# A spectral filter with a gated FFN on one core: scratch rows in another order, forward slabs closer together, Strassen sums on VectorE, and x added to twelve slabs by accumulating DMAs

## The chip, the core and the metric

The kernel runs on one core of one Trainium2 chip. The metric is the device time of one execution in microseconds (us), the median of several runs. The core has five engines with a queue of instructions each: TensorE (PE; its weight loads are listed as PEld), VectorE (DVE), ScalarE (ACT), GpSimd (POOL) and SyncE (SP), which here issues most of the DMAs. An engine works off its own queue in order; a wait of one instruction holds everything behind it on the same engine.

## The reference

`x` has 2048 rows of 640 columns (bf16). It is normalised by row, filtered in the frequency domain and multiplied by a gate from a feed-forward network; `x` is added at the end:

```python
xn = _layernorm(x, axis=-1)
X  = rfft2(xn);  X = X * (w_r + 1j * w_i);  s = irfft2(X, (S, D))      # S = 2048, D = 640, 321 columns kept
g  = silu((gelu(xn @ w_gate) * (xn @ w_up)) @ w_down)                  # F = 1536
return x + s * g
```

## The kernel before

The FFTs are matrix products. The 2048 rows are cut into 16 slabs (`NS`, index `n1`) of 128 rows, row = 16 * n2 + n1. A forward slab is two groups of instructions: `slab_S1` (product over n2 with Tfwd into `pz`, emptied by ScalarE) and, two steps later, `slab_D` (product over the columns with FT into `pd`, emptied by ScalarE into `RZ`), after which SP stores the slab to the DRAM scratch `ZDR` (L604). `load_B2` reads the scratch back in another order, so that the second transform over n1 can run as 64-row products: `s2_in(b)` gives `px`, ScalarE empties it into `xs`, VectorE multiplies it by the two filter tensors W1 and W2 (L659, into the buffers of `RZ`), and `s2_out(b)` gives `pu`, which ScalarE empties into `RX` (L680) and SP stores to the DRAM scratch `UDR` (L683). There are eleven such bursts (`BURSTS`). `load_V` reads `UDR` back (into VY for slabs 0 to 3 and over W2 for the others), and the inverse runs slab by slab: `gather` (L710), `slab_S1i` (pv), `group_Di` for three slabs at a time, `group_cs` and `group_Y` on VectorE, and `finish`, which multiplies a slab by its gate (L788), adds x from `RX` (L789) and lets SP store it (L790). The x rows come from `load_xt`, two slabs at a time, into two halves of `RX`.

The FFN is spread between these parts. `ffn_piece` (L806) is five products of 128x512 into a bank `psg` or `psu`; ScalarE applies gelu (L811) and VectorE multiplies the two (L813, into `UT`). The down product of the four groups of four slabs is done directly (`down_third`, L944) for group 0 and half of group 3, and for groups 1, 2 and half of 3 by a Strassen-Winograd scheme: `w_sum` and `u_sum` (L872, L881) make sums of the operands on VectorE, and `product(g, a, i)` makes seven products (L900) of six matrix multiplies each. What comes out of the banks is added up: on VectorE (L907), by ScalarE copies (L910, L919), and for two of the seven sums on GpSimd. `gated` applies the activation: for groups 1 and 2 by a tanh on ScalarE (L844) and a VectorE instruction (L849), both put off by one product each (`flush`).

The two pools of PSUM banks matter for the order: `psg` and `psu` have two banks each, used in turn by FFN pieces and products; `pz`, `pd`, `px`, `pu` and `pv` share two double banks.

The order of all of this is written out by hand. `back` is a list of 144 steps (FFN pieces, products, down thirds); `put(s, f, ...)` hangs other work behind step s. Steps 36 to 59 are the FFN of group 1, 60 to 71 its products, 72 to 95 the FFN of group 2, 96 to 107 its products, 108 to 131 the FFN of group 3, 132 to 137 its seven products and 138 to 143 its direct part. In the kernel before, `slab_S1` of slab n1 stands behind step `FA[n1]` (29 to 58), `load_B2` behind 60, the first `s2_in` behind 68, the last `s2_out` behind 90, `load_V` behind 91, and the first `slab_S1i` behind 100.

`TB` splits a `u_sum` over the six blocks of UT: the blocks below TB are summed during the FFN, the rest later, for the second half of a group (a = 1) inside the products.

## Time and profile before

| | us |
|---|---|
| median of 3 runs (lowest, highest) | 199.49 (199.12, 199.73) |
| the profiled execution: its own time | 198.94 |
| the profiled execution: its span | 197.2 |

The span is the time from the first to the last record of the profile; the run's own time holds what lies around it as well. The profile shows, by engine, when instructions ran and what they waited for: groups of instructions (busy time, mean ns of one, idle time before), waits (who waited for whom), the chain that ended last, a timeline, windows of time and the DMA issues with their time to landing. The TensorE clock was granted in full over the whole span. Lines such as L806 are lines of the kernel as printed above. The lines that matter stand in the prediction.

### The profile page before, as it was taken

To read this page: it belongs to the slowest core of one execution; us is meant where nothing else is said; L and a number is where in the kernel's file an instruction comes from. 1 tells how busy PE (TensorE), PEld (TensorE's weight loads), DVE (VectorE), ACT (ScalarE), POOL (GpSimd) and SP (SyncE) were. 2 spreads that over 40 slices of the span, in tenths; PEclk is the share of its full clock that TensorE was granted. 3 is DMA by queue.
4 is the path that set the end of the run, shared out by engine and by line. 5 is a ranking of instruction groups with operands and counts; after the bars stand their busy time and mean duration, and the time that the engine had idled before them with its cause. 6 is when DMAs were issued, how large, how long until landed. Compare 5 with 4: busy or idle time off the path is not lost.

```text
span 197.2 us, 4191 instructions
## 1 busy us (share of the span) xinstructions
PE 188.7 (96%) x1496; PEld 116.4 (59%) x1511; DVE 158.4 (80%) x380; ACT 127.6 (65%) x229; POOL 48.9 (25%) x78
## 2 busy tenths in 40 slices
PE   7999999999999999999899999997999999999992
PEld 5798854777555555676433433454765555557672
DVE  7887888989899877697786658566779887978994
ACT  4668567866976666825598878622766738374761
POOL 4448588997210200032200000002120000000310
PEclk9999999999999999999999999999999999999999
DMA  6999999676596773329953222329910416040713
GB/s 162 301 331 362 367 320 188 139 207 208 134 179 126 218 243 104 99 72 317 243 132 103 76 100 100 116 69 257 325 41 28 138 41 195 33 136 15 220 44 94
DMA packets 39653, 32.44 MB, mean 165 GB/s; under 512 B 13264, under 2 KB 38608, under 8 KB 39376
## 3 DMA queue, kind: packets, MB, share of 16 engines
q1 hardware_dynamic: 37568, 29.87, 54.7%
q10 hardware_dynamic: 1968, 0.98, 1.8%
q0 software_dynamic: 96, 1.31, 1.7%
q8 instruction: 12, 0.20, 0.4%
q14 instruction: 9, 0.07, 0.1%
HBM read 19.03 MB, written 7.88 MB: 136 GB/s over the span
## 4 chain that ended last, share of the span: by engine, by line
PE 81%; DVE 8%; DMA 3%; issue 3%; ACT 2%; SPq 1%; DVEq 0%; ACTq 0%
PE psg L806 26%; PE psu L806 25%; PE psu L900 5%; PE psg L900 5%; PE psu L944 3%; PE psg L944 3%; PE pz L565 2%; PE pu L674 2%; PE pv L730 2%; PE pd L596 2%; PE pd L575 2%; DMA VY<-UDR 2%; PE px L647 2%; DMA X<-in_A_x_dram 2%; DVE X L788 1%
## 5 line engine op out<-in xcount | busy, mean ns | idle before, releaser
L806 PE MATMUL psg<-XG,Wg 128*128 128x512 bf16 (+2 forms) x282 | 60.1, 342 | 0.7 <-issue 0.3
L806 PE MATMUL psu<-XG,Wu 128*128 128x512 bf16 (+2 forms) x283 | 60.2, 342 | 0.4 <-issue 0.2
L813 DVE TENSOR_TENSOR UT<-psu,ge 128x512 bf16<-128x512 f32 (+2 forms) x58 | 34.4, 593 | 18.4 <-PE psu L806 16.1
L811 ACT ACTIVATE ge<-psg 128x512 bf16<-128x512 f32 (+2 forms) x58 | 30.3, 523 | 16.8 <-PE psg L806 16.1
L806 PEld LDWEIGHTS <-Wu 128*128 128x128 bf16 x290 | 27.0, 98 | 22.4
L806 PEld LDWEIGHTS <-Wg 128*128 128x128 bf16 x290 | 25.9, 98 | 21.3 <-issue 3.5
L659 DVE TENSOR_TENSOR RZ<-xs,W 128x972 bf16<-128x972 bf16 (+2 forms) x22 | 14.0, 678 | 5.5 <-ACT xs L655 4.7
L900 PEld LDWEIGHTS <-UT 128*128 128x128 bf16 x150 | 14.3, 98 | 5.6 <-issue 0.2
L944 PEld LDWEIGHTS <-UT 128*128 128x128 bf16 x156 | 14.4, 98 | 5.0
L601 ACT CAST RZ<-pd 128x660 bf16<-128x660 f32 x16 | 11.3, 707 | 9.1 <-PE pd L598 9.1
L190 DVE BATCH_NORM_STATS2 st<-X 128x6 f32<-128x320 bf16 x32 | 14.0, 476 | 0.4 <-DMA X<-in_A_x_dram 0.4
L732 ACT CAST W<-pv 128x640 bf16<-128x640 f32 x16 | 11.0, 688 | 5.0 <-PE pv L730 4.8
L755 ACT ACTIVATE W<-pd 128x960 bf16<-128x960 f32 (+2 forms) x14 | 10.0, 778 | 5.1 <-PE pd L579 5.1
L680 ACT CAST RX<-pu 128x486 bf16<-128x486 f32 (+4 forms) x22 | 12.2, 557 | 0.3
L655 ACT CAST xs<-px 128x972 bf16<-128x972 f32 (+2 forms) x11 | 10.3, 935 | 3.2 <-PE px L647 3.2
L944 PE MATMUL psg<-Wd,UT 128*128 128x320 bf16 (+1 forms) x84 | 11.8, 288 | 0.0
L567 ACT CAST GEN<-pz 128x640 bf16<-128x640 f32 x16 | 11.2, 698 | 0.0
L907 POOL TENSOR_TENSOR Tfwd<-Y,XG 128x320 f32<-128x320 f32 x1 | 0.9, 868 | 40.0 <-ACT XG L919 40.0
L844 ACT ACTIVATE th<-Tfwd 128x320 f32<-128x320 f32 x10 | 4.5, 469 | 9.5 <-DVE Tfwd L907 9.5
L907 POOL TENSOR_TENSOR Tfwd<-XG,Tfwd 128x320 f32<-128x320 f32 x1 | 0.9, 857 | 38.3 <-ACT Tfwd L919 38.3
L944 PE MATMUL psu<-Wd,UT 128*128 128x320 bf16 (+1 forms) x72 | 10.3, 290 | 0.0
L761 DVE TENSOR_TENSOR W<-W 128x960 bf16<-128x960 bf16 (+1 forms) x12 | 7.3, 632 | 1.8 <-ACT W L755 1.8
(215 smaller groups left out, 317.1 us busy)
## 6 DMA issues: line engine op xcount, KB each, us to landing
ZDR<-RZ SPq DMA_DIRECT2D x32, 80.2 KB, 2.8
UDR<-RX SPq DMA_DIRECT2D x10, 240.8 KB, 2.4
RX<-in_A_x_dram SPq DMA_DIRECT2D x14, 160.0 KB, 2.6
B<-ZDR SPq DMA_DIRECT2D x8, 240.8 KB, 4.3
W<-UDR SPq DMA_DIRECT2D x4, 481.5 KB, 7.1
X<-in_A_x_dram SPq DMA_DIRECT2D x3, 640.0 KB, 10.0
Wd<-in_B_w_down_dram SPq DMA_DIRECT2D x1, 1920.0 KB, 14.3
out_dram<-VY SPq DMA_DIRECT2D x12, 160.0 KB, 1.8
```

Source lines behind the costliest of these rows:

```text
L190: nc.vector.bn_stats(out=st_n[n1][:, k, :], in_=X[:, n1, 320 * k:320 * k + 320])
L567: nc.scalar.copy(out=Zt[n1], in_=pz)
L601: nc.scalar.copy(out=zd.rearrange("p c (q e) -> p c q e", e=10), in_=pd[:, :, 0:330].rearrange("p c (e q) -> p c q e", q=33))
L655: nc.scalar.copy(out=xs, in_=px[:, :, 0:n * w].rearrange("p k (h l) -> p k h l", l=w))
L659: nc.vector.tensor_tensor(out=pp[-1], in0=xs, in1=WT[:, :, h0:h0 + n, l0:l0 + w], op=ALU.mult)
L680: nc.scalar.copy(out=us[:, :, :, c0:c0 + (w + 1 - m) // 2], in_=pv[:, :, :, m:w:2])
L732: nc.scalar.copy(out=vs, in_=pv)
L806: nc.tensor.matmul(ps, lhsT=WT[:, c, t * P:(t + 1) * P], rhs=xnT[g][:, c, c0:c1_], start=(c == 0), stop=(c == 4))
L811: nc.scalar.activation(out=ges[t], in_=ps, func=ACT.Gelu_apprx_tanh)
L813: nc.vector.tensor_tensor(out=UT[:, t, c0:c1_], in0=ps, in1=ges[t], op=ALU.mult)
L900: nc.tensor.matmul(ps, lhsT=lhs[:, t, :], rhs=rhs[:, t, :], start=(t == 0), stop=(t == 5))
L944: nc.tensor.matmul(ph, lhsT=UT[:, t, j * P:(j + 1) * P], rhs=Wd[:, t, c0:c1_], start=(t == 0), stop=(t == NT - 1))
```

## The change

- The scratch tensors lose their split by odd and even rows: `[2, 2, NS, 64, L]` becomes `[2, NS, P, L]`. A forward slab is stored by one DMA of 128 partitions (two of 64 before), and `load_V` issues four DMAs of 128 partitions (eight of 64 before). The rows of the second transform change places with it: B2 and the `RX` buffers hold the two halves `hh` of a row pair next to each other, and `load_B2` and the `UDR` stores are split by the upper and lower 64 partitions, with runs of 3852 bytes (128 partitions with runs of 1926 bytes before), in the same number of DMAs. In `w_plus` the rows read are every second one, so each of its DMAs moves 16 x 16 rows of 642 bytes (16 contiguous runs of 10272 bytes before). The constants follow (`u64`). The two `RX` buffers of the second transform are used in the other order.
- Forward slabs 8 to 15 stand closer: FA ends at 54 instead of 58, `slab_D` always two steps later. `load_B2` stands behind step 56 (60 before), the first `s2_in` behind 67 (68), the last `s2_out` still behind 90 but two steps after the last `s2_in`, `load_V` still behind 91, the first use of V one step earlier.
- The Strassen sums: products 3 and 4 change places, and all sums are made on VectorE from the bank; the second copy by ScalarE and the two sums on GpSimd go. `TB` is 5 instead of 3, and the sums of the operands stand at other steps.
- `finish` of slabs 0 to 11 (`XA` = 12) leaves out the VectorE add of x: GpSimd issues a DMA that adds x from DRAM to the slab (`accum_op=ALU.add`), and SP's store waits for it. `load_xt` remains for slabs 12 to 15.

```diff
-    ZDR = dram.tile([2, 2, NS, 64, L], BF16)
-    UDR = dram.tile([2, 2, NS, 64, L], BF16)
+    ZDR = dram.tile([2, NS, P, L], BF16)
+    UDR = dram.tile([2, NS, P, L], BF16)
...
     def w_plus(i, hh, lo):
-        u0 = lo * 32 + hh * 16
-        nc.sync.dma_start(out=WT[p0:p0 + 61:4, lo].rearrange("p h l -> p (h l)"),
-                          in_=sp[:, u0:u0 + NS, :].rearrange("k h l -> k (h l)"))
+        u0 = lo * 32 + hh
+        nc.sync.dma_start(out=WT[p0:p0 + 61:4, lo], in_=sp[:, u0:u0 + 31:2, :])
...
     def slab_D(n1):
-        for a in range(2):
-            nc.sync.dma_start(out=ZDR[a, :, n1].rearrange("c p l -> p c l"), in_=zd[a:P:2, :, 0:L])
+        nc.sync.dma_start(out=ZDR[:, n1].rearrange("c p l -> p c l"), in_=zd[:, :, 0:L])
...
+    def turned(t, lo, h0, h1):
+        return t[64 * lo:64 * lo + 64, 2 * h0:2 * h1, :].rearrange("p k l -> p (k l)")
+
+    def rows(t, lo, h0, h1):
+        v = t.rearrange("c n (z a k) l -> a (c n z) (k l)", a=2, z=2)
+        return v[lo, :, 2 * h0 * L:2 * h1 * L]
...
     def load_B2():
-            for hh in range(2):
-                nc.sync.dma_start(out=B4[:, hh, h0:h1, :], in_=zv[:, hh, h0:h1, :])
+            for lo in range(2):
+                nc.sync.dma_start(out=turned(B2, lo, h0, h1), in_=rows(ZDR, lo, h0, h1))
...
     def s2_out(b):
-        us = st_b["u"][:, h0 // 3 % 2, :, 0:n * L].rearrange("p k (h l) -> p k h l", l=L)
+        ut = st_b["u"][:, (h0 // 3 + 1) % 2, 0:2 * n, :]
+        us = ut.rearrange("p (h k) l -> p k h l", k=2)
...
-            for hh in range(2):
-                nc.sync.dma_start(out=uv[:, hh, h0:h0 + n, :], in_=us[:, hh, :, :])
+            for lo in range(2):
+                nc.sync.dma_start(out=rows(UDR, lo, h0, h0 + n), in_=turned(ut, lo, 0, n))
...
     def load_V():
             for c in range(2):
-                for a in range(2):
-                    nc.sync.dma_start(out=V[a:P:2, :, c * L:c * L + L],
-                                      in_=UDR[a, c, n0:n1].rearrange("n p l -> p n l"))
+                nc.sync.dma_start(out=V[:, :, c * L:c * L + L], in_=UDR[c, n0:n1].rearrange("n p l -> p n l"))
...
     def finish(n1):
-        nc.vector.tensor_tensor(out=Y, in0=Y, in1=xts[n1][:, sl], op=ALU.add)
+        if n1 < XA:
+            nc.gpsimd.dma_start(out=Y, in_=xv[:, n1, sl], accum_op=ALU.add)
+        else:
+            nc.vector.tensor_tensor(out=Y, in0=Y, in1=xts[n1][:, sl], op=ALU.add)
...
-    TB = 3
+    TB = 5
...
     def product(g, a, i):
-                    (A(1, 0), TS[:, 2]), (S[:, 0], TS[:, 0]), (A(0, 1), B4[:, :, 1, 1, :]), (A(1, 1), TS[:, 3]))[i]
+                    (S[:, 0], TS[:, 0]), (A(1, 0), TS[:, 2]), (A(0, 1), B4[:, :, 1, 1, :]), (A(1, 1), TS[:, 3]))[i]
...
         elif i == 3:
-            d["p7"], d["u3"] = temp(), temp()
-            nc.scalar.copy(out=d["p7"], in_=ps)
-            add(nc.gpsimd, d["u3"], d["p1"], d["p7"])
+            d["u4"] = temp()
+            add(d["u4"], d["p1"], ps)
         elif i == 4:
-            d["u4"] = temp()
-            add(nc.vector, d["u4"], d["p1"], ps)
-            add(nc.gpsimd, d["p7"], d["u4"], d["p7"])
+            c, d["u3"] = temp(), temp()
+            add(c, d["u4"], ps)
+            gated(g, j + 1, 1, c, True)
+            add(d["u3"], d["p1"], ps)
...
-    for i, at in enumerate((51, 52, 54, 56)):
+    for i, at in enumerate((51, 52, 53, 54)):
         put(at, w_sum, i)
-    put(52, u_sum, nc.vector, 1, 0, 0, 3)
-    put(57, u_sum, nc.vector, 1, 1, 0, 3)
-    put(59, u_sum, nc.vector, 1, 0, 3, 6)
...
+    for g, at in ((1, 56), (2, 92), (3, 128)):
+        put(at, u_sum, nc.vector, g, 0, 0, TB)
+        if g in STR:
+            put(at + 1, u_sum, nc.vector, g, 1, 0, TB)
+        put(at + 3, u_sum, nc.vector, g, 0, TB, 6)
-    FA = (29, 31, 33, 35, 37, 39, 41, 43, 45, 47, 49, 51, 53, 55, 57, 58)
+    FA = (29, 31, 33, 35, 37, 39, 41, 43, 44, 46, 47, 49, 50, 51, 53, 54)
     for n1 in range(NS):
-        put(min(FA[n1] + 2, 45 + n1), slab_D, n1)
+        put(FA[n1] + 2, slab_D, n1)
         put(FA[n1], slab_S1, n1)
-    z_end = F0 + 30
+    z_end = FA[NS - 1] + 2
...
-    sb = z_end + 8
+    sb = 67
...
-    put(sb + 22, s2_out, len(BURSTS) - 1)
-    sb += 23
+    put(sb + 23, s2_out, len(BURSTS) - 1)
+    sb += 24
     put(sb, load_V)
-    vs0 = sb + 8
+    vs0 = sb + 7
...
-    put(vs0 - 2, load_xt, 0)
-    put(vs0 + 4, load_xt, 1)
+    for pair in range(XA // 2, 8):
+        put(vs0 + 4 * pair, load_xt, pair)
```

More of the change, by code (lines that the diff above doesn't have):

```diff
@@ L119, in w_minus @@
         p0 = hh * 64 + 1
[L120 removed]
+        u0 = lo * 32 + hh
         if u0 == 0:
[L122 removed]
+            nc.sync.dma_start(out=WT[p0:p0 + 61:4, lo, 1:NS, :], in_=sp[:, 126:97:-2, :])
             nc.sync.dma_start(out=WT[p0:p0 + 61:4, lo, 0, :], in_=sp[:, 64, :])
         else:
[L125 removed]
+            nc.sync.dma_start(out=WT[p0:p0 + 61:4, lo, :, :], in_=sp[:, 128 - u0:97 - u0:-2, :])
     def w_twin(i, pm):
@@ L647, in s2_in @@
                     nc.tensor.matmul(ps, lhsT=MG[r, kind, 0, :],
-                                     rhs=B2[r, 16 * hh + h0 + i:16 * hh + h0 + j, l0:l0 + w], start=(i == 0),
+                                     rhs=B2[r, 2 * (h0 + i) + hh:2 * (h0 + j) - 1 + hh:2, l0:l0 + w], start=(i == 0),
                                      stop=(j == n))
@@ L660, in s2_in @@
         st_b[b] = pp
-    uv = UDR.rearrange("a c n (z k h) l -> (a c n z) k h l", z=2, k=2)
     def s2_out(b):
@@ L713, in gather @@
             st_c[("r", n0 + k)] = vr[:, k, :]
+    XA = 12
     xts = {}
@@ L906, in product @@
         j = 2 * a
-        add = lambda eng, out, in0, in1: eng.tensor_tensor(out=out, in0=in0, in1=in1, op=ALU.add)
+        add = lambda out, in0, in1: nc.vector.tensor_tensor(out=out, in0=in0, in1=in1, op=ALU.add)
         if i == 0:
@@ L1117, in build @@
             put(min(d + (5 + k if n == 3 else 2), vs0 + 41), finish, n0 + k)
-            if (n0 + k) % 2 and 1 < (n0 + k + 3) // 2 < 8:
-                put(min(d + (5 + k if n == 3 else 2), vs0 + 41), load_xt, (n0 + k + 3) // 2)
     warm_pe(21)
```

29 lines of the change are left out of this document (8 added, 21 removed).

## The prediction

> **What bounds the kernel now.** I read the page of the profile first: the share of each engine, the 40 slices, and the chain of work that ended last.
>
> ```profile
> span 197.2 us, 4191 instructions
> PE 188.7 (96%) x1496; PEld 116.4 (59%) x1511; DVE 158.4 (80%) x380; ACT 127.6 (65%) x229; POOL 48.9 (25%) x78
> PE   7999999999999999999899999997999999999992
> PE 81%; DVE 8%; DMA 3%; issue 3%; ACT 2%; SPq 1%; DVEq 0%; ACTq 0%
> ```
>
> TensorE is busy 188.7 of 197.2 us and holds 81% of the chain. The number of its matrix products does not change, so the change can only win back what TensorE stands still, 8.5 us, of which start and end take most: the slices dip at the first, at slice 28 (133 to 138 us) and at the last. Next come TensorE's own waits (us in total, times, longest).
>
> ```profile
> PE pv L730 <- DMA VY<-UDR: 1.3, 1, 1.3
> PE pu L674 <- ACT RX L680: 0.8, 2, 0.5
> ```
>
> Two waits stand out, and the chain in order of time (start, length, what) shows both places. The first is the entry to the second transform:
>
> ```profile
> 94.86 0.46 PE pu L674 x6
> 95.37 0.50 DVE Tfwd L907
> 95.95 0.47 ACT th L844
> 96.42 0.85 ACT xs L655
> 97.30 1.23 DVE RZ L659 x2
> ...
> 99.91 0.86 ACT xs L655
> ...
> 101.88 0.62 PE pu L674 x8
> ...
> 105.10 0.41 PE pu L674 x8
> ...
> 108.10 0.41 PE pu L674 x8
> ```
>
> From 105.10 on a burst and its two FFN halves take 3.00 us. The three bursts from 94.86 to 105.10 took 10.24 us, so 10.24 - 9.00 = 1.24 us are lost here. The chain says why: a VectorE sum of the Strassen products (L907) ends late, ScalarE stands in order behind the tanh that needs it, and so empties px and pu late. The second place is the load of V:
>
> ```profile
> 130.63 0.58 SPq L699
> ...
> 132.57 3.33 DMA VY<-UDR
> ...
> 136.03 0.53 PE pv L730 x4
> 136.56 0.81 PE psu L900 x6
> ```
>
> SP issues four loads one after the other, and only the fourth, under way at 132.57, ends the wait. Then the tail (start, length, engine, line):
>
> ```profile
> 192.66 0.83 PE L944 MATMUL psg<-Wd,UT 128*128 128x128 bf16 x12
> 193.53 0.28 ACT L841 ACTIVATE XG<-psg 128x128 bf16<-128x128 f32 x1 [0.34 <-PE psg L944]
> 194.23 0.22 DVE L789 TENSOR_TENSOR X<-X,RX 128x128 bf16<-128x128 bf16 x1
> ```
>
> TensorE ends at 193.5 and VectorE's last add at 194.45: the last 1 us is the inevitable last piece, and the store follows. A lighter VectorE does not shorten it. What can be won is thus 1.24 + 1.3 us and crumbs: about 3 us is the ceiling.
>
> **The change part by part, against the profiled execution (span 197.2, its own time 198.94; the median of the runs is 199.49, 0.55 above).**
>
> *Load of V.* Four VY loads of 64 rows become two of 128 rows, and four W2 loads two. Issue time on SP, by the tile view (min, median, max in ns), and, from the list of DMA issues, size and time to landing:
>
> ```profile
> L699 SPq DMA_DIRECT2D VY<-UDR x4: 605/616/646, 130.6 to 132.6; - x4
> UDR<-RX SPq DMA_DIRECT2D x10, 240.8 KB, 2.4
> UDR<-RX SPq DMA_DIRECT2D x2, 80.2 KB, 3.9
> ```
>
> Two issues fewer are 2 x 0.62 = 1.24 us less before the last VY load is under way. SP starts them when the last UDR stores have landed. The two small stores took 3.9 us against 2.4 for bigger ones, so I read 1.5 us as queueing behind the burst before; that burst's stores now go one step earlier, while the small ones stay at their step (90). Bounds of this: 0 to 1.5 us earlier. Against both, the first use of V moves one step forward (vs0 is 98, not 99): one product, 0.81 us, less cover. TensorE's wait becomes 1.3 + 0.81 - 1.24 = 0.87 us with no help from the stores and vanishes with 0.9 of it. A gain of 0.4 to 1.3; I take 1.0, near the upper end, since the step that now separates the stores is about half of the 3.00 us pace and covers most of the 0.9. What is late next is the gather on VectorE (L710), which waits for the same load and is issued one step earlier too; behind it stand two product sums whose banks TensorE needs only two products later, so this costs nothing.
>
> [...]
>
> *Entry to the second transform.* Forward slabs 8 to 15 come up to four steps earlier, so the B2 load is called at step 56 instead of 60 and s2_in(0) at 67 instead of 68; s2_in(1) and s2_out(0) come at step 70, ahead of the last two products rather than behind them. The load gains some three steps on its first reader, so it should no longer be the reader's limit. What remains is VectorE. Rows of one instruction each (count, busy us, mean ns, idle before):
>
> ```profile
> L907 DVE TENSOR_TENSOR Tfwd<-Tfwd,psg 128x320 f32<-128x320 f32 x4 | 1.9, 479 | 0.1
> L881 DVE TENSOR_TENSOR XG<-UT 128x384 bf16<-128x384 bf16 x6 | 2.1, 353 | 0.1
> L789 DVE TENSOR_TENSOR VY<-VY,RX 128x640 bf16<-128x640 bf16 x12 | 5.9, 492 | 0.4
> ```
>
> Each set of seven products has seven sums on VectorE instead of five: five sets, ten sums, 10 x 0.48 = 4.8 us more, of which 4 x 0.48 = 1.9 fall before this entry. Five ScalarE copies and ten GpSimd sums go. The GpSimd sums were not free to VectorE:
>
> ```profile
> 86.11 0.86 POOL L907 TENSOR_TENSOR FT<-Tfwd,Y 128x320 f32<-128x320 f32 x1 [17.39 <-ACT Y L919]
> 86.18 1.01 DVE L881 TENSOR_TENSOR UT<-UT 128x384 bf16<-128x384 bf16 x1
> ...
> 92.53 1.91 DVE L659 TENSOR_TENSOR RZ<-xs,W 128x972 bf16<-128x972 bf16 x2 [0.80 <-DMA B<-ZDR]
> 92.96 0.95 POOL L907 TENSOR_TENSOR Y<-Tfwd 128x320 f32<-128x320 f32 x1 [3.94 <-ACT Tfwd L919]
> ```
>
> Under a GpSimd sum the 0.35 us instruction took 1.01 and the 1.23 us pair 1.91: 0.66 + 0.68 = 1.3 us come back. The u_sums keep their elements, but with TB at 5 less of them lies inside the products: three of 384 columns become three of 128, at most 0.35 each and say 0.4 in all. Net on VectorE before the entry: +1.9 - 1.3 - 0.4 = +0.2 us. ScalarE has two copies less in its queue, and px(1) and pu(0) are emptied while sums are still to come, not behind the last tanh. Bounds: if neither the GpSimd relief nor the new order helps, 1.9 - 0.4 = 1.5 us lost; if the entry runs at the steady pace, 1.24 won. I take 0.6 won, since the row that names the wait (pu on ScalarE's RX) is the one that the new order attacks.
>
> In the second group the same sums meet two VectorE idles at the V loads, and four product banks stand between VectorE and TensorE; in the third, VectorE has lost more than it gained (next part). Both at nothing; without that cover a set costs 2 x 0.48 us.
>
> *x by an accumulating DMA.* Twelve VectorE adds of 0.49 (5.9 us) and twelve x loads go; twelve GpSimd DMAs come. TensorE shows no wait on VectorE there, so 5.9 us of VectorE are worth nothing by themselves: they pay for the sums above. The DMA itself has no row; the nearest are GpSimd's copies of W2:
>
> ```profile
> L129 POOL DMA_DIRECT2D W<-W x2 | 1.4, 686 | 12.2 <-DMA ZDR<-RZ 12.2
> W<-W POOLq DMA_DIRECT2D x2, 642.0 KB, 4.2
> 183.52 0.49 DVE L789 TENSOR_TENSOR VY<-VY,RX 128x640 bf16<-128x640 bf16 x1
> 189.59 5.32 SPq L790 DMA_DIRECT2D out_dram<-X  x8
> ```
>
> SP's store of a slab now waits for its DMA, and everything behind it on SP too: the x loads for slabs 12 to 15, which have over 10 us to spare, and the last stores. The last accumulated slab is multiplied by 183.5. With three issues of 0.69 and a landing of 4.2 it is home at 189.8, as the stores of slab 12 begin. Bounds: nothing, to 1 us if a landing takes twice 4.2 (194, when SP still has three stores to issue). I take 0.
>
> *Scratch rows in another order.* The forward store is one DMA for two; SP gains time nobody waits for. w_plus reads 16 x 16 rows of 642 bytes in place of 16 long ones. Windows of 1 us (window, length, then busy time of PE, PEld, DVE, ACT and POOL, PE clock, DMA share, GB/s), and the first reader of Tfwd:
>
> ```profile
> 26.00:27.00 1.00, 1.00 (x7) 0.46 (x5) 1.00 (x4) 0.23 (x1) 0.92 (x4) 1.00 1.00 394
> 29.00:30.00 1.00, 1.00 (x7) 0.44 (x5) 0.97 (x4) 1.00 (x2) 1.00 (x1) 1.00 1.11 214
> ...
> 36.83 5.15 SPq L361 DMA_TRANSPOSE Tfwd<-Tinv  x4
> ...
> 40.36 0.39 PE L565 MATMUL pz<-Tfwd,RX 128*128 128x128 bf16 x4
> ```
>
> Full DMA engines move 394 GB/s of long rows and 214 while the w rows run. Four w_plus of 160 KB are 1.6 us at the one and 3.0 at the other: up to 1.4 us more in front of the transposes of Tfwd, which are issued 3.5 us ahead of their first use. Bounds 0 to 1.4; I take 0.1.
>
> Sum: -1.0 - 0.6 + 0.1 = -1.5 us: span 195.7, profiled run 197.4, median 199.49 - 1.5 = 198.0.
>
> **The rivals.**
> 1. *Both waits go altogether.* 1.24 + 1.3 plus some tenths of scattered issue gaps: -2.8, 196.7. For it: after the entry the pace is steady. Against it: px must still be emptied by a ScalarE that waits for tanh inputs.
> 2. *The gain is hidden.* The 64-row stores land no sooner than before, or later, so that of the V load only 0.4 is left, and the entry stays as it was: -0.3, 199.2. For it: the use of V was moved forward by as much as two of the loads gave. [...]
> 3. *VectorE becomes the bound in the products (slower).* Place: the entry at 95 to 102. If VectorE reaches RZ of the third burst more than about 1 us later than now, pu(2) waits for it, and behind pu(2) the FFN. Price: 1.5 us as above, less what V gains shrink to (0.4 of it, as the later end of the stage holds the last stores too), and 0.3 to 0.5 in the second group: +1.4, 200.9. For it: VectorE's sums lie on the chain already. Against it: the collisions with GpSimd.
> 4. *The accumulating DMAs are slow (slower).* From a landing of about 8 us on, slabs 9 to 11 hold SP beyond 191 and the last stores queue: at 10 us some 2 us, less the 1.5 gained: 200.1. For it: SP serves in order. Against it: 160 KB is a quarter of what took 4.2 us.
>
> [...]
>
> **How the numbers follow.** Forecast 0.52, rival 1 0.14, rival 2 0.15, rival 3 0.12, rival 4 0.07. A measurement here tells no change up to 0.3%, 0.6 us. Faster: 0.52 + 0.14 = 0.66; within: 0.15; slower: 0.19. The forecast's own range is 196.9 to 198.9. Down to 196.3 most of rival 1 is in; up to 200.2 rival 2 and the milder half of the slower ones: 196.3 to 200.2.
>
> **What would show it.** Right: TensorE's wait at pv on VY under 0.4 us with two VY issues in front; the first three pu intervals summing to under 9.8 us; no GpSimd sum and no 1.0 us L881; VectorE's share near 79%. Wrong: SP's wait on UDR longer than before (rival 2); TensorE waiting on RZ or for a product bank (rival 3); out stores waiting on accumulating DMAs past 190 us (rival 4); a TensorE gap near 40 us (w rows). If nothing of this moves and the time does, the reasons are wrong.

## The result, and the profile after

| | changed kernel | kernel before, same chip | ratio (95% interval) |
|---|---|---|---|
| first measurement | 197.05 us median (196.43 to 197.27, 4 runs) | 199.31 us (199.00 to 199.73, 4 runs) | 0.988 (0.985 to 0.9911) |
| second measurement | 196.47 us (195.93 to 196.62, 6 runs) | 198.71 us (198.18 to 200.51, 29 runs) | 0.988 (0.985 to 0.991) |

The changed kernel is faster by 2.25 us, both times; the forecast was 1.5. Executions over 1.5% longer than the fastest of the same kernel are left out of every ratio here, but not out of the medians, and the one profile of v_both is of such an execution, so that its stages are not in the table below. The changed kernel's first profiled execution took 197.07 us (span 195.2), its second 196.40 (span 194.5). From the page of the first:

```profile
span 195.2 us, 4162 instructions
PE 187.4 (96%) x1496; PEld 115.6 (59%) x1511; DVE 154.5 (79%) x379; ACT 126.6 (65%) x224; POOL 50.5 (26%) x80
PE   7899999999999999999999999999999999999992
PE 80%; DMA 10%; SPq 3%; DVE 3%; ACT 2%; issue 1%; DVEq 0%; ACTq 0%
```

The dip of slice 28 is gone from TensorE's row, and VectorE has gone from 8% of the chain to 3%. The share of DMA rose from 3% to 10% (5% in the second profile), as the chain now passes through the B2 load, though TensorE shows no wait for it. TensorE's waits of the same profile (us in total, times, longest):

```profile
PE pt L973 <- DVE X L218: 0.8, 1, 0.8
PE pu L674 <- ACT RX L681: 0.4, 1, 0.4
PE pz L563 <- DMA Tfwd<-Tinv: 0.4, 1, 0.4
PE pv L730 <- DMA VY<-UDR: 0.3, 1, 0.3
```

The wait for V fell from 1.3 to 0.3 us and that at pu from 0.8 to 0.4. The wait at pz is new. The one at pt at the very start looks like a loss of 0.8 us and is none, as the timelines of TensorE of the first and of the second profile of the changed kernel show (start, length, engine, line):

```profile
1.18 3.83 PE L609 MATMUL psg<-GEN 128*128 128x256 bf16 x21 [1.18 <-DVE eps L229]
5.77 0.54 PE L973 MATMUL pt<-ident,X 128*128 128x128 bf16 x5 [0.77 <-DVE X L218]
```

```profile
1.17 4.66 PE L609 MATMUL psg<-GEN 128*128 128x256 bf16 x21 [1.17 <-DVE eps L229]
5.80 0.72 PE L973 MATMUL pt<-ident,X 128*128 128x128 bf16 x5
```

The same 21 warming products took 3.83 us in one execution and 4.66 in the other, and the first transposition starts at 5.8 in both: the wait is what the products left over.

To find where the 2.25 us come from, I cut TensorE's timeline at five instructions that every kernel here has: the first matmul of the forward transform (pz), the first product of each FFN group that is multiplied out in products (P1, P2, P3), and the last group of matmuls. The rows for the kernel before (the first and the last of the five stand in the prediction: 40.36 and 192.66):

```profile
81.83 0.98 PE L900 MATMUL psg<-Wd,UT 128*128 128x320 bf16 x6
...
130.45 0.98 PE L900 MATMUL psg<-Wd,UT 128*128 128x320 bf16 x6
...
178.63 0.98 PE L900 MATMUL psg<-Wd,UT 128*128 128x320 bf16 x6
```

and for the second profile of the changed kernel:

```profile
40.51 0.38 PE L563 MATMUL pz<-Tfwd,RX 128*128 128x128 bf16 x4
...
82.28 0.98 PE L903 MATMUL psg<-Wd,UT 128*128 128x320 bf16 x6
...
129.57 0.98 PE L903 MATMUL psg<-Wd,UT 128*128 128x320 bf16 x6
...
176.36 0.98 PE L903 MATMUL psg<-Wd,UT 128*128 128x320 bf16 x6
...
190.06 0.83 PE L946 MATMUL psg<-Wd,UT 128*128 128x128 bf16 x12
```

Differences of such rows give the length of each stage. The experiments of the next section are in the table too, each read in the same way from its own profile.

| kernel | span | to pz | pz to P1 | P1 to P2 | P2 to P3 | P3 to last group | rest |
|---|---|---|---|---|---|---|---|
| before | 197.2 | 40.36 | 41.47 | 48.62 | 48.18 | 14.03 | 4.5 |
| changed, first profile | 195.2 | 40.69 | 41.78 | 47.30 | 47.34 | 13.70 | 4.4 |
| changed, second profile | 194.5 | 40.51 | 41.77 | 47.29 | 46.79 | 13.70 | 4.4 |
| rows_only | 196.7 | 40.16 | 41.48 | 48.95 | 47.47 | 14.03 | 4.6 |
| acc_only | 196.7 | 40.48 | 41.48 | 48.63 | 47.66 | 14.03 | 4.4 |
| old_slots | 196.4 | 40.86 | 41.48 | 48.84 | 47.07 | 13.71 | 4.4 |
| rows_steps | 194.7 | 40.33 | 41.78 | 47.63 | 46.59 | 13.70 | 4.7 |
| old_sums | 194.5 | 40.37 | 41.77 | 47.64 | 46.59 | 13.71 | 4.4 |
| x_vector | 194.3 | 40.20 | 41.78 | 47.30 | 46.59 | 13.79 | 4.6 |
| v_halves | 195.3 | 40.88 | 41.78 | 47.30 | 47.45 | 13.71 | 4.2 |
| late_bursts | 195.2 | 40.59 | 41.77 | 47.39 | 47.29 | 13.71 | 4.4 |
| both_fixes | 194.9 | 40.49 | 41.77 | 47.29 | 47.27 | 13.71 | 4.4 |
| fixes2 | 194.5 | 40.40 | 41.78 | 47.30 | 46.88 | 13.71 | 4.4 |

Two columns repeat to a few hundredths of a microsecond: pz to P1 and P1 to P2. With the new steps the D of slab 15 stands before P1 rather than behind it; that moves 0.31 us from the one to the other (41.78 - 41.47) and is no gain. So the entry to the second transform, which lies between P1 and P2, won 48.62 - 0.31 - 47.30 = 1.01 us. P2 to P3, with the load of V, won 0.84 us in the first profile and 1.39 in the second; its floor, reached three times, is 46.59. P3 to the last group won 0.33. The start differs by scatter and by the wait at pz.

Nearly all of the 1.01 us lies at two places. One is the first burst, px(0), and no list of waits names it, since the row merges the products around the stop. TensorE's timeline, before and in the first profile of the changed kernel:

```profile
90.38 0.79 PE L647 MATMUL px<-B,MG 64*64 64x162 bf16 x5
91.10 0.99 PE L900 MATMUL psg<-X,UT 128*128 128x320 bf16 x6
```

```profile
89.90 0.41 PE L649 MATMUL px<-B,MG 64*64 64x162 bf16 x5
90.24 0.99 PE L903 MATMUL psu<-X,RX 128*128 128x320 bf16 x6
```

From px(0) to the product behind it are 0.72 us before and 0.34 after: 0.38 won. By the single records of the trace the third of the five products starts at 90.77, and the second B2 load, issued at 87.8, lands 2.9 us later, at 90.73: the kernel before did wait for that load. In acc_only, which has the same loads, px(0) takes 0.74. The other place is the distance of the first pu's, here in the first profile of the changed kernel:

```profile
93.02 0.58 PE L674 MATMUL pu<-RZ,N 64*64 64x162 bf16 x10
...
96.58 0.57 PE L674 MATMUL pu<-RZ,N 64*64 64x159 bf16 x10
...
100.19 0.63 PE L674 MATMUL pu<-RZ,N 64*64 64x486 bf16 x8 [0.45 <-ACT RX L681]
...
103.25 0.57 PE L674 MATMUL pu<-RZ,N 64*64 64x477 bf16 x8
```

From pu(0) to pu(3) are 10.23 us in both kernels (94.70 to 104.93 before, by the timeline), but the work between is not the same: the changed kernel has the last two products (1.63 us) there and one FFN half (1.08) less. At the steady pace of 3.00 this takes 9.00 us before and 9.00 + 1.63 - 1.08 = 9.55 after, so 1.23 were lost before and 0.68 after: 0.55 won. From pu(3) to the next are 2.99 us again.

### The profile page after: what moved, and what is told of

It is laid out like the page before. It is cut to its first block, busy times and chain, and to the rows that moved or that the text cites. A ratio compares the mean times of both kernels' runs of the same rounds, so it can differ in the third digit from the quotient of the medians.

```text
span 195.2 us, 4162 instructions
## 1 busy us (share of the span) xinstructions
PE 187.4 (96%) x1496; PEld 115.6 (59%) x1511; DVE 154.5 (79%) x379; ACT 126.6 (65%) x224; POOL 50.5 (26%) x80
## 4 chain that ended last, share of the span: by engine, by line
PE 80%; DMA 10%; SPq 3%; DVE 3%; ACT 2%; issue 1%; DVEq 0%; ACTq 0%
PE psu L809 25%; PE psg L809 24%; PE psg L946 5%; PE psg L903 4%; PE psu L946 4%; DMA B<-ZDR 4%; PE psu L903 3%; DMA VY<-UDR 2%; PE pz L563 2%; PE pd L573 2%; SPq L624 2%; PE pv L730 2%; PE pd L594 2%; PE pu L674 2%; DMA Tfwd<-Tinv 1%
## 5 line engine op out<-in xcount | busy, mean ns | idle before, releaser
L809 PEld LDWEIGHTS <-Wu 128*128 128x128 bf16 x290 | 26.1, 98 | 22.5 <-issue 3.4
L809 PEld LDWEIGHTS <-Wg 128*128 128x128 bf16 x290 | 26.5, 98 | 20.2 <-issue 0.2
L790 POOL DMA_DIRECT2D VY<-in_A_x_dram x12 | 10.6, 1035 | 95.3 <-PE psu L809 74.3
L661 DVE TENSOR_TENSOR RZ<-xs,W 128x972 bf16<-128x972 bf16 (+2 forms) x22 | 13.3, 648 | 9.8 <-ACT xs L657 9.5
L207 POOL TENSOR_TENSOR rst<-ve,mhalf 128x1 f32<-128x1 f32 (+1 forms) x6 | 5.5, 913 | 11.6 <-DVE ve L205 11.6
L903 PE MATMUL psu<-Wd,UT 128*128 128x320 bf16 x48 | 7.8, 300 | 0.0
```

The lines of the kernel that those rows point to most:

```text
L661: nc.vector.tensor_tensor(out=pp[-1], in0=xs, in1=WT[:, :, h0:h0 + n, l0:l0 + w], op=ALU.mult)
L790: nc.gpsimd.dma_start(out=Y, in_=xv[:, n1, sl], accum_op=ALU.add)
L809: nc.tensor.matmul(ps, lhsT=WT[:, c, t * P:(t + 1) * P], rhs=xnT[g][:, c, c0:c1_], start=(c == 0), stop=(c == 4))
L903: nc.tensor.matmul(ps, lhsT=lhs[:, t, :], rhs=rhs[:, t, :], start=(t == 0), stop=(t == 5))
```

## The experiments

A ratio's interval here is about 0.3% to each side, 0.6 us. Differences between two variants that are smaller than that rest on the stages of the profiles, not on the times.

**v_halves.** The V loads in 64-row halves again:

```diff
-                nc.sync.dma_start(out=V[:, :, c * L:c * L + L], in_=UDR[c, n0:n1].rearrange("n p l -> p n l"))
+                for a in range(2):
+                    nc.sync.dma_start(out=V[a:P:2, :, c * L:c * L + L],
+                                      in_=UDR[c, n0:n1, a::2].rearrange("n p l -> p n l"))
```

> The changed kernel with one edit: each of the four V loads is split again into two of 64 rows, as in the kernel before (eight issues by SP). The prediction's term (two VY issues fewer are worth 2 x 0.62 = 1.24 us): TensorE's wait at pv on VY rises from 0.34 to about 1.6 us, and the time by 1.2 us, from 197.05 to 198.3. The rival from the second trace (the bytes of VY, 321 KB, take 3.9 us after the last issue whatever their number; what helped is only that the first issue stands 1.55 us earlier against the products): the last VY row lands 5.2 to 5.4 us after the first issue as now, the wait stays under 0.6 us, and the time within 0.3 us of 197.05.

Measured: 197.09 us against 198.62 before, ratio 0.9924 (0.989 to 0.9959); wait at pv 0.6 us. By its median it lies where the rival put it; against the kernel before of the same chip it is 0.9 us worse than the changed kernel, with an interval of 0.6 or more. The rival's reason fell with the other runs. The rows of V by tile (min, median, max in ns; then landing in us after an issue) in v_halves, in the first profile of the changed kernel and in x_vector, whose V load is that of the changed kernel:

```profile
L700 SPq DMA_DIRECT2D VY<-UDR x4: 610/616/677, 128.7 to 130.7; - x4
...
DMA to landing us min/median/max: 2.7/2.8/3.1
```

```profile
L699 SPq DMA_DIRECT2D VY<-UDR x2: 383/552/721, 128.3 to 128.8; - x2
...
DMA to landing us min/median/max: 3.1/3.9/4.8
```

```profile
L699 SPq DMA_DIRECT2D VY<-UDR x2: 381/530/678, 128.0 to 128.4; - x2
...
DMA to landing us min/median/max: 3.3/3.6/3.8
```

The last VY row is home at the latest 130.7 + 3.1 - 128.7 = 5.1 us after the first issue with four issues, and 128.4 + 3.8 - 128.0 = 4.2 us with two; the first profile of the changed kernel, with 128.78 + 4.77 - 128.34 = 5.2 by its chain of waits, was a bad draw of the same load. Over all profiles here this time is 4.1 to 5.2 us with two issues (ten profiles, median 4.2) and 5.0 to 5.6 with four (before, acc_only, v_halves and v_both). Two issues fewer are worth about 1 us of landing. What the kernel feels of it is less, because V then comes up to 0.5 us before it is needed.

**late_bursts.** The last burst, and with it the stores of burst 9, one step later:

```diff
-    AT = (0, 3, 5, 7, 9, 11, 13, 15, 17, 19, 21)
+    AT = (0, 3, 5, 7, 9, 11, 13, 15, 17, 19, 22)
```

> The changed kernel with one edit: s2_in of the last burst and s2_out of burst 9, whose two stores of 240.8 KB to UDR follow, one step later (step 89 instead of 88), as in the kernel before; the last small stores stay at step 90. If the step that separates the stores starts the V load earlier (1.55 us in the two traces), about one FFN half of it, 0.8 to 1.5 us, is given back: wait at pv on VY 1.1 to 1.8 us, time 197.9 to 198.5. The rival (the small stores set the start of the load, and landed sooner for another reason, the 64-row form of the stores): wait under 0.6 us, time within 0.3 us of 197.05.

Measured: 197.20 us against 198.62, ratio 0.992 (0.9891 to 0.9949); wait at pv 0.3. SP's first V issue stands at 129.29, 0.46 us before P2 (129.75); with the changed steps it stands 1.4 us before P2 in the first profile (128.34 and 129.77) and 1.0 in the second (128.55 and 129.57). Over all profiles it stands 0.12 us behind P2 and 0.07 before it in the two kernels with the old rows (before and acc_only), 0.2 to 0.6 before it in the four with the new rows and the late stores (rows_only, old_slots, late_bursts, v_both), and 1.0 to 1.5 before it in the other eight. So the step of the stores starts the load about 0.9 us earlier, as the first theory says, and the new form of the rows about 0.4, where the rival has a part. From the list of DMA issues of the changed kernel:

```profile
UDR<-RX SPq DMA_DIRECT2D x10, 240.8 KB, 3.0
UDR<-RX SPq DMA_DIRECT2D x2, 80.2 KB, 2.3
```

The big stores take longer than before (2.4 us, and 3.5 in rows_only), but the two small ones, the last that the load waits for, are home sooner than in the kernel before (3.9; 2.8 in rows_only). The wait that the first theory named (1.1 us or more) was not seen: V landed 129.73 + 3.74 - 129.29 = 4.2 us after its first issue, where the first profile of the changed kernel had 5.2.

**v_both.** The two edits above in one kernel.

> The changed kernel with both causes of the earlier V undone at once: the V loads in 64-row halves, and the last burst with the stores of burst 9 one step later; the first use of V stays at step 98. By the prediction's sum the wait is 1.3 + 0.81 = 2.1 us. Each of the two alone brought the stage from the first product of group 2 to the first of group 3 to 47.45 and 47.29 us, against 46.59 without any wait and 46.8 to 47.3 in the changed kernel. If the two add up behind a margin of some 0.5 us: stage 48.0 to 48.7, wait at pv 1.3 to 2.1, time 0.8 to 1.6 us over the changed kernel. Rival (the scatter of the transfers is all there is): stage at or under 47.6, time within 0.4 us of it.

Measured: 197.61 us against 198.73, ratio 0.9938 (0.9915 to 0.996). The five executions that the ratio counts (196.84 to 197.82) have a median of 197.43, 1.0 us over the second measurement of the changed kernel and inside what the first theory gave. By the ratios the first edit alone costs 0.9, the second 0.8 and both 1.15 us: less than the sum, though with intervals of this size the runs can't tell. The stage that the theory named, 48.0 to 48.7 us from P2 to P3, could not be read: the profiled execution, of 199.94 us, waits 1.9 us at pv and shows something else, told in the last section.

**old_sums.** product() of the kernel before in the changed kernel, of which the core is

```diff
-            d["u4"] = temp()
-            add(d["u4"], d["p1"], ps)
+            d["p7"], d["u3"] = temp(), temp()
+            nc.scalar.copy(out=d["p7"], in_=ps)
+            add(nc.gpsimd, d["u3"], d["p1"], d["p7"])
...
-            add(c, d["u4"], ps)
-            gated(g, j + 1, 1, c, True)
-            add(d["u3"], d["p1"], ps)
+            add(nc.vector, d["u4"], d["p1"], ps)
+            add(nc.gpsimd, d["p7"], d["u4"], d["p7"])
```

> The changed kernel with one edit: product() as in the kernel before, with two GpSimd sums and one more ScalarE copy in each set of seven, two VectorE sums fewer, and the old order of products 3 and 4; the steps and the splitting of the u_sums stay. By the prediction's count (2 x 0.48 us less on VectorE in each set, but 0.66 to 0.68 us more for each VectorE instruction that runs under a GpSimd sum) the two nearly cancel: within 0.4 us of 197.05, with VectorE instructions of 1.0 us and over seen under the GpSimd sums. The rival (the collisions and the later emptying of px and pu were what made the entry to the second transform slow): the first pu intervals together 0.5 us longer or more, time 197.6 to 198.3.

Measured: 196.51 us, ratio 0.9909 (0.9875 to 0.9943). P1 to P2 is 47.64 us against 47.30: the new sums are worth 0.34 us at the entry. The timelines of GpSimd and VectorE in this profile show the price of the old ones once more, a pair of 1.93 us that takes 1.22 in the changed kernel:

```profile
92.90 0.90 POOL L910 TENSOR_TENSOR Y<-Tfwd 128x320 f32<-128x320 f32 x1 [4.97 <-DVE Tfwd L910]
93.88 0.86 POOL L910 TENSOR_TENSOR Tfwd<-FT,Tfwd 128x320 f32<-128x320 f32 x1
```

```profile
93.90 1.93 DVE L661 TENSOR_TENSOR RZ<-xs,W 128x954 bf16<-128x954 bf16 x2 [0.43 <-ACT xs L657]
```

The 0.34 us lie inside what the prediction's count allowed (0.4) and have the rival's sign; they stand between pu(0) and pu(3), which are 10.57 us apart here. The times don't show them: the median is 0.5 us under the 197.05 of the first measurement, and level with the second. In the second and third groups the sums change nothing: P2 to P3 is at its floor with the old ones as with the new.

**x_vector and acc_only.** x by VectorE in the changed kernel (XA = 0 and the x loads as before), and x by the accumulating DMA in the kernel before:

```diff
-        nc.vector.tensor_tensor(out=Y, in0=Y, in1=xts[n1][:, sl], op=ALU.add)
+        if n1 < 12:
+            nc.gpsimd.dma_start(out=Y, in_=xv[:, n1, sl], accum_op=ALU.add)
+        else:
+            nc.vector.tensor_tensor(out=Y, in0=Y, in1=xts[n1][:, sl], op=ALU.add)
```

> The changed kernel with one edit: x added by VectorE for all slabs, its loads issued by SP as in the kernel before; no accumulating DMA. The prediction costs the accumulating DMA at nothing, since TensorE never waited for VectorE there: within 0.3 us of 197.05, VectorE about 5.9 us busier. The rival (the twelve VectorE adds of 0.49 us delay the group sums and product sums behind them now that each set has two more): 0.5 to 1.5 us slower, with TensorE waits for product banks or for SS in the third group. A third way (the issues of 0.9 us on GpSimd and the stores waiting for them cost something): 0.3 to 0.6 us faster.

> The kernel before with one edit: x added to slabs 0 to 11 by the accumulating DMA of GpSimd (two x loads are left). Theory (VectorE held up nothing behind the V load): within 0.3 us of the kernel before. Rivals: 0.5 us or more faster if the twelve adds or the ten x loads on SP were in the way of something, 0.5 us or more slower if the issues and the waiting stores cost.

Measured: x_vector 196.58 us, ratio 0.9889 (0.9855 to 0.9923); acc_only 198.85 against 198.71, ratio 0.9994 (0.9968 to 1.0021). By its median x_vector is 0.47 us under the first measurement of the changed kernel, as the third way had it, but only 0.1 from the second one (after_again, below), so that no gain is left. Taken out or put in alone, the accumulating DMA moves nothing that these runs can tell. In acc_only, P2 to P3 is 0.52 us shorter than in the kernel before with the same V load (wait at pv 0.7 in place of 1.3), so the 1.3 us on which the prediction built looks like a high draw too.

**rows_only.** The new order of the rows with the steps, the sums and the x of the kernel before.

> The scratch rows in the new order and all transfers that follow from it, with the steps, the sums and the x of the kernel before. Theory (two VY issues fewer bring V home 1.0 to 1.2 us earlier, the rest of the gain comes from the steps): wait at pv 0.1 to 0.4 us instead of 1.3, entry to the second transform as before, so 1.0 us (0.8 to 1.3) under the kernel before. Rival (64-row transfers with long rows are slower on their way, so V starts later): wait 0.8 us or more, within 0.5 us of the kernel before. If the whole gain is in the rows: 2 us under it.

Measured: 198.46 us against 198.71, ratio 0.9989 (0.9965 to 1.0013). The time is the rival's, the reason is not: V starts no later, but 0.40 us before P2 (0.12 behind it in the kernel before). The wait at pv is 0.6, and P2 to P3 0.7 us shorter than in the kernel before. What this wait is put down to is not V but VectorE's gather (L709), which the prediction took at nothing. The timelines of VectorE and GpSimd:

```profile
134.88 0.82 DVE L709 COPY vr<-VY 128x128 bf16<-128x128 bf16 x2 [0.47 <-DMA VY<-UDR]
```

```profile
134.69 0.86 POOL L910 TENSOR_TENSOR Tfwd<-XG,Tfwd 128x320 f32<-128x320 f32 x1 [38.32 <-ACT Tfwd L922]
```

The two copies take 0.82 us instead of the 0.30 of the changed kernel, and the second goes on as a GpSimd sum ends at 135.55: by the timelines, another collision with an old sum. The entry pays for the gain, P1 to P2 is 0.33 longer. The rows, from the timeline of TensorE and the list of DMA issues of rows_only, and from that list of the kernel before:

```profile
90.26 0.40 PE L649 MATMUL px<-B,MG 64*64 64x162 bf16 x3
91.22 0.40 PE L649 MATMUL px<-B,MG 64*64 64x486 bf16 x2 [0.57 <-DMA B<-ZDR]
91.55 0.99 PE L903 MATMUL psg<-X,UT 128*128 128x320 bf16 x6
```

```profile
B<-ZDR SPq DMA_DIRECT2D x8, 240.8 KB, 5.1
```

```profile
B<-ZDR SPq DMA_DIRECT2D x8, 240.8 KB, 4.3
```

The loads of the same size now fill 64 rows each instead of 128 and land in 5.1 us instead of 4.3; the second half of the first burst, which reads rows 64 to 127, waits for them. The row names 0.57 us, but px(0) takes 1.29 us up to the next product where it takes 0.34 undisturbed: 0.95 lost, against 0.38 in the kernel before. The distances of the pu's give 0.3 of it back (9.92 us from pu(0) to pu(3)); my guess is that VectorE catches up while TensorE stands, which no run shows. The landings are longer by a fifth; their runs are twice as long too, and no run tells which of the two makes them so.

**old_slots.** The changed kernel with the forward slabs, the B2 load, the bursts and the last stores at the steps of before:

```diff
-    FA = (29, 31, 33, 35, 37, 39, 41, 43, 44, 46, 47, 49, 50, 51, 53, 54)
+    FA = (29, 31, 33, 35, 37, 39, 41, 43, 45, 47, 49, 51, 53, 55, 57, 58)
-        put(FA[n1] + 2, slab_D, n1)
+        put(min(FA[n1] + 2, 45 + n1), slab_D, n1)
-    z_end = FA[NS - 1] + 2
+    z_end = 60
-    sb = 67
+    sb = 68
-    put(sb + 23, s2_out, len(BURSTS) - 1)
-    sb += 24
+    put(sb + 22, s2_out, len(BURSTS) - 1)
+    sb += 23
```

> The changed kernel with the forward slabs, the B2 load, the bursts and the last stores at the steps of the kernel before (B2 load at step 60, first burst at 68, stores of burst 9 at 89, last ones at 90); rows, sums, x and the first use of V at step 98 stay. Theory: the entry gives back 0.5 to 0.6 us (px(1) and pu(0) once more behind the last sums, now seven of VectorE), and V waits 0.3 to 0.6 us more: 0.8 to 1.2 us slower than the changed kernel. Rival (the entry gained by the sums, not by the steps): within 0.4 us of it. A third way (the new sums need the new steps: seven VectorE sums stand in front of the bursts' products): 1.5 us or more slower.

Measured: 198.19 us, ratio 0.9968 (0.9947 to 0.9989), 1.7 us over the changed kernel; the spans differ by 1.9. Of that P1 to P2 is 48.84 - 0.31 - 47.29 = 1.24 us, P2 to P3 0.28 and the start 0.35. Most of the 1.24 stands at the first burst: px(0) begins 0.13 us late and takes 1.29 us up to the next product (91.02 to 92.31) as in rows_only, together 1.08. The pu that waits 0.54 us for ScalarE explains little, for from pu(0) to pu(3) the loss is 0.74 us here and 0.68 in the changed kernel. So the steps do carry the entry, but by the earlier B2 load rather than by px(1) and pu(0) standing ahead of the last products, as the theory had it; what that order would be worth if the load came in time, no run shows. By its time the run falls under the third way, whose reason doesn't hold, since with the old steps the new sums still win a little, 48.95 - 48.84 = 0.11.

**rows_steps.** Rows and steps alone, old_sums and x_vector in one kernel.

> The changed kernel with both VectorE parts undone: the sums of product() as in the kernel before (two on GpSimd), and x added by VectorE for all slabs; the rows in the new order and the new steps stay. Theory (rows and steps carry the gain; the sums are worth 0.3 us at the entry to the second transform, the accumulating DMA nothing): from the first product of group 1 to the first of group 2 47.6 us as with the old sums alone (47.3 in the changed kernel, 48.3 before without slab 15's D), time within 0.5 us of the changed kernel. Rival (each of the two parts pays for the other: with twelve adds and without relief in the sums VectorE becomes the bound): 1 us or more slower than the changed kernel, with TensorE waiting for banks in the second or third set of products.

Measured: 196.87 us against 198.73, ratio 0.9914 (0.9893 to 0.9934), all stages as the theory says. So of the 2.25 us rows and steps bring 1.86; the rows by themselves bring 0.25, which the interval of rows_only does not tell from nothing. The steps without the new rows were not run, so how much of the 1.86 needs the rows is not shown.

**after_again.** The changed kernel once more.

> The changed kernel as it is, beside the other runs of this call. In the first profile of it V landed 5.2 us after its first issue and TensorE waited 0.34 us; in the two kernels with other sums or another x, whose V load is the same, it landed about 4.2 us after and TensorE did not wait. If that is scatter of the transfers, a second profile shows a landing of 4.2 to 5.2 us and a wait of 0 to 0.34, and the time stays within 0.4 us of the variants with the old sums or with x on VectorE. If the accumulating DMAs or the VectorE sums cost something, this kernel stays 0.4 us or more slower than those.

Measured: 196.47 us, no wait at pv by name, landing of VY by its row 3.2/3.5/3.8 us, level with old_sums and x_vector (196.51 and 196.58). It was scatter. The 0.20 us by which P2 to P3 still exceeds its floor here stand almost wholly at the gather: the pv that reads it starts 0.40 us behind the ones before it (132.84 to 133.24), 0.22 in x_vector (132.54 to 132.76).

**both_fixes and fixes2.** An attempt to take the scatter of V and of Tfwd away:

```diff
-            put(a + ((1, 2, 4)[k] if n == 3 else 1), slab_S1i, n0 + k)
+            put(a + ((2, 3, 4) if i == 0 else (1, 2, 4) if n == 3 else (1,))[k], slab_S1i, n0 + k)
-    for i, places in enumerate(((8, 9, 10, 11, 12, 13, 14, 15, 30, 31), (32, 32, 35, 35, 38, 38, 41, 41, 50, 50))):
+    for i, places in enumerate(((8, 9, 10, 11, 27, 28, 29, 30, 42, 42), (32, 32, 35, 35, 38, 38, 41, 41, 50, 50))):
-    put(40, w_edge, 0)
+    put(46, w_edge, 0)
```

and in fixes2 also `d = a + (7 if i == 0 else 6)` for the first group of the inverse.

> The changed kernel with two small moves: slabs 0 and 1 of the inverse transform use V one step later (offsets 2 and 3 instead of 1 and 2), and the four w loads of the real part that stand last go behind the transposes of Tfwd on SP (steps 27 to 30, the twin copies and the edge with them to 42 and 46). Theory (what is left of waits is scatter of the V load, 0 to 0.75 us, and of the Tfwd transposes, 0 to 0.5 us): no wait at pv and at pz, stage between the first products of groups 2 and 3 46.6 us in every profile, time 0.3 to 0.6 us under the changed kernel. Rivals: the moved w loads hold up the forward stores or the transposes of slabs 8 to 11 on SP (0.5 us or more slower), or slabs 0 and 1 one after the other make pv wait for its copy (same time).

> As both_fixes, with the first group of the inverse (its products with FI) one step later too, so that the copy of slab 2 again has three steps before it: both_fixes showed no wait at pv and pz, but 0.5 us at pd for ScalarE's copy of a slab. Theory: no wait at pv, pz or pd; from the first product of group 2 to that of group 3 46.6 us; span 194.0 to 194.4, time 195.7 to 196.1, 0.4 us or more under the changed kernel and level with the best executions of both_fixes (195.72 to 196.10). Rival: the later first group delays the Y of slabs 0 to 2 and with them nothing that TensorE reads, so only the scatter of the rest is left and the median does not move from 196.0; or group 1's slabs now stand too close behind and pd waits there instead (196.4 or more).

Measured: both_fixes 196.01 us against 198.73, ratio 0.987 (0.9849 to 0.9891); fixes2 196.46 against 198.80, ratio 0.9879 (0.9856 to 0.9902). The waits at pv and pz are gone in both, but in both_fixes the next link shows itself, ScalarE's copy of slab 2 (timeline of TensorE):

```profile
139.37 0.87 PE L573 MATMUL pd<-FI,W 128*128 128x160 bf16 x10 [0.53 <-ACT W L732]
```

With it P2 to P3 is 47.27 in both_fixes, not the 46.6 that was expected. fixes2 has no named wait left there and P2 to P3 at 46.88, and is no faster than the changed kernel: 196.46 where 195.7 to 196.1 were expected. No version here beats the changed kernel by more than a measurement can tell.

## Why the prediction was right, and where its sizes were off

Forecast were 1.5 us, won 2.25. By the stages these are 1.01 at the entry, 0.84 to 1.39 with the load of V and 0.33 at the last D of the inverse, less some 0.1 for the w rows.

*The load of V, taken at 1.0 (0.4 to 1.3).* Right in kind and about in size: 0.84 and 1.39 us in the two profiles of P2 to P3, and 1.0 us given back by the times when both causes are undone. Of its two terms, the issues (1.24) measure about 1 us of landing and the step of the stores (most of 0.9) about 0.9 us of start. The new form of the rows gave another 0.4 of start, where rival 2 had it lose: the big stores did land later, but the small ones sooner. What the working lacked is the spread of its starting number: the wait of 1.3 us is 0.7 with the same load in acc_only, and the same two issues need 4.2 us in one execution and 5.2 in another. With the wait a draw from such a range, "0.87 us with no help from the stores" was too exact. In late_bursts V still starts 0.58 us earlier against P2 than in the kernel before (0.46 ahead instead of 0.12 behind); 0.87 - 0.58 = 0.29, and it waited 0.30, but one profile with such scatter is no proof. With the 47.66 of acc_only for a start the gain of this stage is 0.32 and 0.87. That the gather on VectorE costs nothing did not hold: it is the named wait in rows_only, and in both profiles of the changed kernel the pv that reads the gathered rows starts 0.40 us behind the ones before it instead of 0.22.

*The entry, taken at 0.6 (1.5 lost to 1.24 won).* 1.01 us were won, 0.38 of them at a place that the sum leaves out: the 1.24 were counted from pu(0) on, and the stop at the first burst stands ahead of it. The prediction wrote that the B2 load "should no longer be the reader's limit", which held, and put no price on it. It was worth more than the 0.38, since the new loads of 64 rows need the earlier call: with the old steps the first burst loses 0.95 us (rows_only, old_slots), with the new ones nothing.

The distances of the pu's, which the 0.6 was meant for, brought 0.55. So the size came out, but the reason only in part. The term that was mis-sized is VectorE's balance, "+0.2 us" of new load before the entry: exchanged for the old sums in the same steps, the new ones win 0.34. The order of px(1) and pu(0), which the prediction gave as its reason, is left with 0.21 at most. That the forecast came so near here is partly luck.

The prediction set a test, three pu intervals under 9.8 us in sum, that does not compare like with like: they take 10.23 with the two products and without one FFN half. With the work that the prediction had in mind they take 10.23 - 1.63 + 1.08 = 9.68, and the test is just met.

*Sums in the second and third groups, at nothing.* Right: 46.59 us in P2 to P3 and 13.7 from P3 to the last group with either kind.

*Not foreseen: 0.33 us from P3 to the last group.* The last D of the inverse (TensorE's timeline, before and in the second profile of the changed kernel):

```profile
186.21 0.46 PE L575 MATMUL pd<-FI,W 128*128 128x160 bf16 x4 [0.15 <-ACT W L732]
```

```profile
183.62 0.45 PE L573 MATMUL pd<-FI,W 128*128 128x160 bf16 x4
```

Before, it waited for the copy of slab 15: it starts 1.14 us behind the product ahead of it (185.07), where the distance is 0.82 in the first profile of the changed kernel (183.55 to 184.37), nearly the whole 0.33. In the new steps there is one step more between the two (vs0 is 98, and the D follows at 4 steps, not 3). All kernels of the table with this edit have 13.7 to 13.8, those without it 14.03. The prediction named the moved step only as lost cover of the V load.

*The accumulating DMA, at nothing.* Right, and for the reason given. From the list of DMA issues and the groups of the changed kernel:

```profile
VY<-in_A_x_dram POOLq DMA_DIRECT2D x12, 160.0 KB, 4.0
```

```profile
L790 POOL DMA_DIRECT2D VY<-in_A_x_dram x12 | 10.6, 1035 | 95.3 <-PE psu L809 74.3
```

An issue takes GpSimd some 0.9 us (10.6 / 12) instead of the 0.69 taken. A landing of 4.0 us stands beside the 4.2 taken and is half of the 8 at which rival 4 begins. By the first profile GpSimd issues the last one at 180.3, three microseconds ahead of the 183.5 from which the prediction counted, and SP starts on the stores of slabs 12 to 15 at 186.13.

*The w rows, at 0.1 (0 to 1.4).* The wait for Tfwd is 0.36 us in the first profile of the changed kernel, and there is none in the second or in the kernel before; over the ten profiles that have the new rows at the old place, it is 0.36, 0.30, 0.24, 0.17 and six times none: 0.11 on average.

*The rivals.* Rival 2 is half right in rows_only, where the gain is hidden, though by the B2 loads of 64 rows and a gather under a GpSimd sum and not by the stores that the rival named; the steps and the sums take this away. Rival 3 has its sign turned round: in the new steps VectorE's sums cost less. Rival 1's sum (2.8) is nearly what the second profile shows (spans 197.2 and 194.5), though the pu wait of 0.4 us is still there, and 0.33 us at the last D and 0.38 at the first burst came from places that it did not count.

## What to carry to other kernels

A wait on a transfer in one profile is a draw: here the same load landed 4.2 or 5.2 us after its issue, so look at a second profile before a term is built on it, and compare stages between fixed instructions rather than waits. Compare the starts of neighbouring rows as well, for a merged row of products can hide a stop that no list of waits names. A layout that halves the number of some transfers can make others slower: the B2 loads went from 4.3 to 5.1 us, and without moving their readers' steps next to nothing was won. When a consumer is moved a step, look at every reader behind it: the smallest gain here, that of the last D, came from a step that had been counted as a cost.

## What the runs showed of the hardware that was not expected

In the profiled execution of v_both TensorE stood still for 1.67 us at a stretch, and then ran at half clock. Windows of 1 us (window, length, busy time of PE, PEld, DVE, ACT and POOL, granted clock, DMA share, GB/s):

```profile
134.00:135.00 1.00, 0.00 (x0) 0.00 (x0) 0.00 (x0) 0.00 (x0) 0.00 (x0) 1.00 0.79 197
135.00:136.00 1.00, 0.81 (x8) 0.59 (x9) 0.87 (x6) 0.19 (x1) 0.00 (x0) 1.00 1.11 335
136.00:137.00 1.00, 1.00 (x7) 0.67 (x6) 1.00 (x5) 0.50 (x1) 0.00 (x0) 0.51 1.10 335
...
138.00:139.00 1.00, 1.00 (x5) 0.61 (x4) 0.09 (x1) 0.53 (x2) 0.00 (x0) 0.50 1.14 308
139.00:140.00 1.00, 1.00 (x8) 0.64 (x6) 0.89 (x2) 0.35 (x1) 0.00 (x0) 0.78 1.14 298
140.00:141.00 1.00, 1.00 (x12) 0.77 (x11) 0.85 (x2) 0.39 (x2) 0.00 (x0) 1.00 0.54 143
```

The clock is 0.50 for some 3.4 us, from 136.0 to 139.4, which by an estimate from these windows costs half of that, 1.7 us: with the wait of 1.9 that is nearly all of the 4.0 us by which P2 to P3 (129.68 to 180.27) exceeds its floor there. The profiled execution of the kernel before, with its 1.3 us, keeps its clock in the same place (a window of 2 us):

```profile
134.00:136.00 2.00, 0.75 (x7) 0.38 (x4) 0.29 (x2) 0.42 (x2) 0.86 (x1) 1.00 0.95 221
```

That the stop brought the half clock is argued from their order alone, and one profile shows it: TensorE goes on at 135.19 with the full clock, and the half clock begins at 136.0. What a stop between the 1.3 us of the kernel before and the 1.67 us here does isn't measured, nor that one of 1.3 us always leaves the clock alone: two executions of the kernel before, of 201.42 and 201.86 us, had a mean granted clock of 0.989 and 0.988, as this one had 0.99, and the record holds no profile of them.
